# A gated scan with a two-level mixture of experts on one core: units' work due earlier, two jobs' staged weights asked for ahead of rows

## The chip, the cores and the metric

The kernel runs on one core of a Trainium2 chip. The time is the device time of one execution in microseconds (us), as the median of the runs; TensorE (PE in the profile), VectorE (DVE), ScalarE (ACT), GpSimd (POOL) and SyncE (SP, which only issues transfers here) work side by side and wait for each other by semaphores. PEld is TensorE's weight load, which runs beside the matmuls.

## The reference

A linear recurrence over time, per batch and channel, makes the tokens; each token is then sent to one of 16 experts (4 groups of 4, the largest logit in both steps), and the expert's two-layer network is weighted by the two softmax values.

```
x, f_logit: (4, 3648, 256)   lower_bound: (256)
w_group (256, 4)  w_expert (4, 256, 4)  w1 (4, 4, 256, 1024)  w2 (4, 4, 1024, 256)
f = lower_bound + (1 - lower_bound) * sigmoid(f_logit)
h = f[:, t] * h + (1 - f[:, t]) * x[:, t];  y[:, t] = h          # 14592 tokens of 256
g = argmax(y @ w_group);  e = argmax(y @ w_expert[g])
out = softmax(y @ w_group)[g] * softmax(y @ w_expert[g])[e] * (relu(y @ w1[g, e]) @ w2[g, e])
```

## The kernel before

**Units.** The 14592 tokens are cut into 29 units of 512 (the last one of 256), numbered 0 to 28. A unit's work is: a load of 1 MB (`p1_load`, into one of four `zt` tiles; units 4 to 7 use two `st` tiles instead), a tanh and two affine steps on ACT (L219, L229), one gate on DVE (L245, or L266 for some early units), two scans on DVE (L256), transposes back to rows on PE (L284) and their copies on ACT, router matmuls on PE (L303), a transpose of the logits (L316), and routing: a chain of some twenty short DVE instructions per pair of units (L330 to L389, and L655 to L706 for the choice of experts), which ends in `posi`, the place of each token in its expert's list. GpSimd then scatters the rows into the lists in DRAM (`xs`, L393).

**Jobs.** While later units are still being made, 16 A jobs (A0 to A15) each take 2 to 5 tiles of 128 tokens from the list that is fullest at a given unit (`CHOOSE`, `EARLY`: the unit at which the job's rows are cut, and its tiles). 16 B jobs later do what is left of every expert. The fifth job of the title is A4, the sixth A5, the eighth A7.

- A0 to A3 (`RAW` = 4) are raw: their weights go into `w` tiles and are used as f32 (L1071 for the first layer, L1110 for the second), 16 + 16 matmuls of 256 columns; DVE has nothing to do for them but ACT has the relus (L1074).
- From A4 on weights are staged: four loads of 512 KB go into `st` tiles (eight of them, `STG_BUFS`; `job_weights`, L963), and `job_split` makes a high f16 part on ACT (L971) and a low bf16 part on DVE (L973, called a split here). Rows come into `xr` tiles (six of them; L946), are transposed on PE (L1033) and split on ACT and DVE (L1042, L1043). The first layer is three matmuls for each block (L1097 to L1099) into `ps_m`, evicted by ACT (`hh`, L1102) and DVE (`hl`, L1103); the second layer (L1129) reads `hh` and `hl`.
- A4 and A5 have 2 tiles each and are cut at unit 10, A6 has 3 and is cut at 12, A7 has 3 and is cut at 14. Units are counted into the lists up to the cut, and their scattered rows must have landed before a job's rows are loaded.

**What sets the order.** Once the first jobs start, the units' work stands in a queue of small pieces (`bgq`). After each step of a job `bg_step` takes pieces from it at a rate: for every entry (work, mark) in the list `due`, the pieces still missing to the mark divided by the work left to that point, and the largest of these. Work is counted in steps: a raw or 2-tile job has 10, a 3-tile job 19. `marks[u]` is the place in the queue behind which job rows that are cut at unit u have been asked for. Before, `due` has an entry for every job: the mark of a job's rows is due about half a job before the job ahead of it ends; of A6 (mark 12) at 45, of A7 (mark 14) at 55, where the fourth job ends at 40. The queue of SP keeps the order in which the program asks; on PE, DVE and ACT the build's scheduler sets the order after the first job's start from the order written. `early_rows(u)` asks for the rows of the jobs cut at u; `fetch_to(n)` asks for weights until n pieces (four for each job) have been asked for; each job's preparation asks for some pieces itself, up to two ahead.

Of the kernel before, what the change touches and what calls it, by code (L numbers as in the profile page):

```python
# [22 lines left out]
EARLY = [(4, 2), (6, 2), (8, 2), (8, 2), (10, 2), (10, 2), (12, 3), (14, 3),  # L23
         (16, 4), (18, 4), (20, 4), (22, 5), (24, 5), (26, 5), (28, 5), (28, 5)]
# [11 lines left out]
RAW = 4  # L36
# [17 lines left out]
def gated_scan_moe(ctx: ExitStack, tc, zx, lower, wroute, wexp, out, S):  # L54
# [391 lines left out]
    def p1_thunks(us, groups, parts):  # L446
# [54 lines left out]
        for u in us + [us[-1] + 1]:  # L501
            seq = []
            if u <= FAST:
# [39 lines left out]
                for m in [m for m, v in ROWS_AT.items() if u == v]:  # L543
                    f = lambda m=m: early_rows(m)
                    f.mark = m
                    put(f)
# [11 lines left out]
                if u == FAST:  # L558
                    f = lambda: None
                    f.mark = "begun"  # L560
                    put(f)
                    for v in [v for v in sorted(cuts) if v <= FAST and v not in ROWS_AT]:
                        f = lambda v=v: early_rows(v)
                        f.mark = v
                        put(f)
# [122 lines left out]
    def blanks():  # L688
        while unblanked:
            j = unblanked.pop(0)  # L690
            m = 1 if EARLY[j.idx][1] == 2 else 2
            sync.dma_start(out=xs_v[NT + j.idx][bass.ds(j.e * LW + (PRE - m * P), m * P), :].rearrange("(p k) c -> p k c", k=m),
                           in_=blank[:, None, :].broadcast_to([P, m, RW]))
# [18 lines left out]
        B.tensor_tensor(out=taken, in0=taken, in1=got, op=ALU.add)  # L712

    def early_rows(u):
        for mac in macros:
            for j in mac:
                if j.kind == "A" and EARLY[j.idx][0] == u and j.idx < NE - 1:
                    job_rows(j)
        ready[0] = True
        if u == EARLY[0][0]:  # L720
            fetch_to(pptr[0] + 8)
# [118 lines left out]
    def make_job(kind, idx):  # L840
        j = Job()
        j.kind, j.idx = kind, idx
        j.len = EARLY[idx][1] * P if kind == "A" else CAPS[idx] if kind == "B" else P
        j.tiles = -(-j.len // P)
        j.chunks, j.pieces, j.cols, j.parts = [], [], [], []
        at = 0
        while at < j.len:
            rest = j.len - at
            if kind == "B":
                w = rest if rest <= UNIT else UNIT if rest >= UNIT + P else UNIT - P  # L850
            else:
                w = 2 * P if rest > 3 * P else P if rest > 2 * P else rest
            n = UNIT // w
            j.cols.append([list(range(c, min(KF, c + n))) for c in range(0, KF, n)])
            j.pieces += [(b, min(2 * P, at + w - b)) for b in range(at, at + w, 2 * P)]
            parts, b = [], at
            while b < at + w:
                m = at + w - b
                g = 1 if m > 64 else 2
                parts.append((b, min(m, P // g), g))  # L860
                b += P // g
            j.chunks.append((at, w))
            j.parts.append(parts)
            at += w
        j.raw = kind == "A" and idx < RAW
        j.wh, j.wl, j.st = {}, {}, {}
        j.hh, j.hl = {}, {}
        j.xh, j.xl = {}, {}
        return j
# [85 lines left out]
    def job_weights(j, i):  # L955
        e = job_e(j)
        if j.raw:
            w = wp.tile([P, 1024], F32, name=f"w{i}")
            sync.dma_start(out=w, in_=wexp[bass.ds(e * P, P), i * 1024:(i + 1) * 1024])
            j.wh[i], j.wl[i] = w[:, 0:512], w[:, 512:1024]  # L960
            return
        st = stg.tile([P, 1024], F32, name="st")
        sync.dma_start(out=st, in_=wexp[bass.ds(e * P, P), i * 1024:(i + 1) * 1024])  # L963
        j.st[i] = st
# [184 lines left out]
    macros = [[make_job("A", e)] for e in range(NE)]  # L1149
# [17 lines left out]
    def first_parts():  # L1167
        out = []
        for (j,), u in zip(macros, PLAN):
            half = {}  # L1170

            def begin(j=j, half=half):
                half[0] = bank("m2")
                raw2(j, 0, 0, range(KF // 2), half[0])
            fs = [lambda j=j: job_xt(j, 0)]
            fs += [lambda j=j, cs=cs: m1_step(j, 0, cs) for cs in j.cols[0]]
            fs += [begin, lambda j=j, half=half: m2_step(j, 0, 0, half[0])]
            out += [(u, f) for f in fs]
        return out

    thunks, marks = p1_thunks(list(range(NU)), GROUPS, first_parts())
# [7 lines left out]
    def bg_to(n):  # L1189
        while done[0] < n:  # L1190
            bg_pop()

    def fetch_to(n):
        while pptr[0] < min(n, len(pieces)):
            j, i = pieces[pptr[0]]
            if j.kind == "A" and j.idx not in picked:
                return
            if j.kind != "A":
                bg_to(marks["order"])
            job_weights(j, i)  # L1200
            pptr[0] += 1
        if ready[0]:
            ready[0] = False
            blanks()
# [33 lines left out]
    def work(mac):  # L1238
        return sum(len(j.chunks) * KF + sum(len(p) for p in j.parts) for j in mac)

    due = []
    at = 0
    for mi, mac in enumerate(macros):
        at += work(mac)
        if mi + 2 < len(macros):
            nxt = macros[mi + 2][0]
            due.append((at - (work(mac) // 2 if mi else 0), marks[EARLY[nxt.idx][0]] if nxt.kind == "A" else marks["order"]))
            if nxt.kind == "A" and nxt.idx >= NE - 2:
                due[-1] = (at - work(mac) // 2, marks["order"])
    now = [sum(work(mac) for mac in macros[:len(PLAN)])]  # L1250
    credit = [0.0]

# [110 lines left out]
```

## Time and profile before

| what | value |
|---|---|
| median of 3 runs (lowest, highest) | 763.11 us (760.62, 766.0) |
| the profiled execution's time | 761.96 us |
| its span, first to last instruction | 760.2 us |
| PE busy | 715.6 us (94%) |
| DVE, ACT, POOL busy | 514.6, 445.9, 296.3 us |
| TensorE clock granted, mean | 0.994 |

Some 1.8 us of the profiled execution lie outside the span. The shares are means over stages: up to about 60 us units alone are made, then the raw jobs run to about 137 us, then the A jobs beside the remaining units, and later jobs alone.

### The profile page before, as it was taken

What the parts mean: (1) busy time and instruction counts of PE and PEld (TensorE: products, weight loads), DVE (VectorE), ACT (ScalarE), POOL (GpSimd) and SP (SyncE); (2) the same over time, 40 slices, a digit from 0 to 9 for tenths busy, and PEclk for the clock granted to TensorE, in tenths of its full rate; (3) what the DMA queues carried; (4) which work ended last, traced back from release to release, by engine and by line L of the source; (5) the groups of instructions that cost most, each with busy time, mean ns of one, the idle gap of its engine ahead of it and who ended that gap; (6) DMA issues with size and microseconds to landing.
All of it is one profiled execution on the core that took longest, in us unless ns stands there. A gap on an engine that the chain in (4) does not pass through costs nothing.

```text
span 760.2 us, 17863 instructions
## 1 busy us (share of the span) xinstructions
PE 715.6 (94%) x6471; PEld 588.0 (77%) x6471; DVE 514.6 (68%) x1086; ACT 445.9 (59%) x827; POOL 296.3 (39%) x314
## 2 busy tenths in 40 slices
PE   3569999998899999999999999999999999999995
PEld 1457888886788888888999676867778886777895
DVE  6899758999799976495556754644644645755660
ACT  6567767887577855454545644544544545655651
POOL 3656267668567764632222121312122121123232
PEclk9999999999999999999999999999999999999998
DMA  8978789989888873657994470617155345655520
GB/s 326 413 255 292 243 351 289 408 316 310 289 258 292 242 211 117 170 146 189 222 241 106 113 189 29 169 43 188 47 155 131 114 133 168 196 174 170 168 65 23
DMA packets 100410, 151.35 MB, mean 199 GB/s; under 512 B 60203, under 2 KB 70206, under 8 KB 97504
## 3 DMA queue, kind: packets, MB, share of 16 engines
q1 hardware_dynamic: 85792, 102.84, 46.1%
q0 software_dynamic: 11408, 30.02, 10.7%
q10 hardware_dynamic: 3120, 17.34, 6.7%
q8 instruction: 51, 0.84, 0.5%
q14 instruction: 39, 0.32, 0.1%
HBM read 112.49 MB, written 37.96 MB: 198 GB/s over the span
## 4 chain that ended last, share of the span: by engine, by line
PE 71%; DVE 11%; issue 8%; DMA 3%; POOL 3%; ACT 2%; another core or an unknown queue 1%; SPq 1%; POOLq 0%; DVEq 0%
PE ps_m L1129 28%; PE ps_m L1099 7%; PE ps_m L1097 7%; PE ps_m L1098 7%; PE ps_m L1110 4%; PE ps_m L1071 4%; PE ps_p L1097 3%; PE ps_p L1098 3%; PE ps_p L1099 3%; PE ps_p L284 3%; POOL out_dram L1143 3%; DVE h L256 2%; DVE w L973 1%; PE ps_p L303 1%; DVE hl L1103 1%
## 5 line engine op out<-in xcount | busy, mean ns | idle before, releaser
L1129 PE MATMUL ps_m<-w,hh 128*128 128x256 f16 (+5 forms) x1260 | 218.9, 268 | 1.3 <-issue 1.3
L1129 PE MATMUL ps_m<-w,hl 128*128 128x256 f16 (+4 forms) x740 | 188.5, 267 | 0.6 <-issue 0.6
L973 DVE TENSOR_TENSOR w<-st,w 128x1024 bf16<-128x1024 f32 x112 | 135.8, 1219 | 68.2 <-ACT w L971 66.7
L393 POOL DMA_INDIRECT xs<-rows,posi x114 | 138.2, 1212 | 87.6 <-ACT rows L288 25.6
L1143 POOL DMA_INDIRECT out_dram<-o,info x67 | 71.6, 1069 | 244.1 <-ACT o L1141 226.6
L1129 PE MATMUL ps_m<-w,rows 128*128 128x256 f16 (+5 forms) x880 | 133.8, 267 | 0.3 <-issue 0.3
L1129 PEld LDWEIGHTS <-hh 128*128 128x128 f16 (+7 forms) x1260 | 117.9, 101 | 15.6 <-issue 3.3
L971 ACT CAST w<-st 128x1024 f16<-128x1024 f32 x112 | 116.1, 1047 | 17.6 <-PE ps_m L1129 12.5
L1097 PE MATMUL ps_m<-xh,w 128*128 128x256 f16 (+9 forms) x494 | 120.4, 256 | 2.5 <-DVE hl L1103 2.4
L1099 PE MATMUL ps_m<-xh,w 128*128 128x256 f16 (+9 forms) x494 | 120.3, 256 | 0.8 <-issue 0.8
L1098 PE MATMUL ps_m<-xl,w 128*128 128x256 bf16 (+9 forms) x494 | 120.3, 256 | 0.0
L1103 DVE SCALAR_TENSOR_TENSOR hl<-ps_m,hh 128x512 bf16<-128x512 f32 (+7 forms) x107 | 71.1, 671 | 40.6 <-ACT hh L1102 24.7
L1098 PEld LDWEIGHTS <-w 128*128 128x128 f16 x800 | 78.3, 98 | 25.3 <-issue 3.7
L1097 PEld LDWEIGHTS <-w 128*128 128x128 f16 x800 | 78.3, 98 | 23.2 <-issue 1.6
L1099 PEld LDWEIGHTS <-w 128*128 128x128 bf16 x800 | 78.3, 98 | 22.8 <-issue 0.4
L1143 POOL DMA_INDIRECT out_dram<-o,meta x47 | 53.4, 1136 | 101.8 <-ACT o L1141 69.1
L1129 PEld LDWEIGHTS <-rows 128*128 128x128 f16 (+4 forms) x880 | 81.6, 101 | 10.0 <-issue 0.6
L1102 ACT ACTIVATE hh<-ps_m 128x512 f16<-128x512 f32 (+7 forms) x107 | 63.3, 594 | 37.1 <-PE ps_m L1099 32.1
L1141 ACT ACTIVATE o<-ps_m,info 128x256 f32<-128x256 f32 (+4 forms) x67 | 31.1, 463 | 91.5 <-PE ps_m L1129 75.8
L1129 PEld LDWEIGHTS <-hl 128*128 128x128 bf16 (+4 forms) x740 | 70.8, 101 | 9.1 <-issue 1.9
L256 DVE TENSOR_TENSOR_SCAN h<-zt,h 128x512 f32<-128x512 f32 (+3 forms) x48 | 56.6, 1191 | 0.5
L1103 DVE SCALAR_TENSOR_TENSOR hh<-ps_p,rows 128x512 bf16<-128x512 f32 (+7 forms) x30 | 17.6, 586 | 45.4 <-ACT rows L1102 45.3
(203 smaller groups left out, 1183.4 us busy)
## 6 DMA issues: line engine op xcount, KB each, us to landing
st<-in_wexp_dram SPq DMA_DIRECT2D x112, 512.0 KB
zt<-in_zx_dram ACTq DMA_DIRECT2D x16, 1024.0 KB
w<-in_wexp_dram SPq DMA_DIRECT2D x16, 512.0 KB
xs<-blank SPq DMA_DIRECT2D x26, 258.0 KB
zt<-in_zx_dram SPq DMA_DIRECT2D x6, 1024.0 KB
st<-in_zx_dram SPq DMA_DIRECT2D x8, 512.0 KB
xr<-xs SPq DMA_DIRECT2D x12, 258.0 KB
xr<-xs SPq DMA_DIRECT2D x16, 129.0 KB
```

The source lines that it names most:

```text
L256: sn = nc.vector.tensor_tensor_scan(out=h[:, k, c0 - a:c1 - a], data0=ff[:, k, c0 - a:c1 - a], data1=uu[:, k, c0 - a:c1 - a], initial=init ...
L393: sc = nc.gpsimd.indirect_dma_start(out=xs_v[G["t0"] + t][:, :], out_offset=bass.IndirectOffsetOnAxis(ap=R["posi"][:, t:t + 1], axis=0), i ...
L971: nc.scalar.copy(j.wh[i], j.st[i])
L973: nc.vector.tensor_tensor(out=j.wl[i], in0=j.st[i], in1=j.wh[i], op=ALU.subtract)
L1097: nc.tensor.matmul(po, w1_at(j.wh, k, c), xh[:, k], start=(k == 0), stop=False)
L1098: nc.tensor.matmul(po, w1_at(j.wh, k, c), xl[:, k], start=False, stop=False)
L1099: nc.tensor.matmul(po, w1_at(j.wl, k, c), xh[:, k], start=False, stop=(k == KD - 1))
L1102: eviction[0] = nc.scalar.activation(hi, pv, AF.Relu).ins
L1103: nc.vector.scalar_tensor_tensor(out=h_at(j.hl[ch], cs, slice(0, w)), in0=pv, scalar=0.0, in1=hi, op0=ALU.max, op1=ALU.subtract)
L1129: nc.tensor.matmul(pm[i * q:i * q + n, 0:dw], h_at(h[ch], [c], ts)[:, 0], w2_at(w, c)[:, i * dw:(i + 1) * dw], start=(c == 0 and s == 0), ...
L1141: nc.scalar.activation(o[s, 0:dw], pm[s, 0:dw], AF.Copy, scale=lt.bitcast(F32)[s, r, 1:2])
L1143: nc.gpsimd.indirect_dma_start(out=out_v[out_n[0]].rearrange("n (g d) -> (n g) d", g=g), out_offset=bass.IndirectOffsetOnAxis(ap=lt[s, r, ...
```

## The change

Two additions. In `early_rows`, at the cut of the fifth job (unit 10), weights are asked for up to piece 24, which is all four pieces of A4 and A5, before their rows. And `due` gets one more entry: mark 14, behind which A7's rows have been asked for, is due at the end of the fourth job (40 steps in place of 55), which raises the rate at which pieces of the units' work are taken during the raw jobs. Nothing is computed that was not computed before, and no instruction of the jobs or the units is added or left out. Lines from 715 on are two higher in the changed file, those from 1250 on three.

```diff
     def early_rows(u):
+        if u == EARLY[RAW][0]:
+            fetch_to(4 * (RAW + 2))
         for mac in macros:
             for j in mac:
                 if j.kind == "A" and EARLY[j.idx][0] == u and j.idx < NE - 1:
...
             if nxt.kind == "A" and nxt.idx >= NE - 2:
                 due[-1] = (at - work(mac) // 2, marks["order"])
+    due.append((sum(work(mac) for mac in macros[:RAW]), marks[EARLY[RAW + 3][0]]))
     now = [sum(work(mac) for mac in macros[:len(PLAN)])]
```

How the order moves. On SP, at the loads of the fifth job's rows (`st` is a staged weight piece, `xr` the rows, `posA` the place of the list's cut), before:

```order
L963 DMA st<-in_wexp_dram 128x1024
L896 ISA
L896 TENSOR_LOAD posA
L896 ISA x2
L946 ISA
L946 REGISTER_ALU
L946 DMA xr<-xs 128x258
```

and now, five more pieces of weights ahead of the same load (the last three of them shown):

```order
L965 ISA
L965 DMA st<-in_wexp_dram 128x1024
L965 ISA
L965 DMA st<-in_wexp_dram 128x1024
L965 ISA
L965 DMA st<-in_wexp_dram 128x1024
L898 ISA
L898 TENSOR_LOAD posA
L898 ISA x2
L948 ISA
L948 REGISTER_ALU
L948 DMA xr<-xs 128x258
```

Before, three of the eight pieces of A4 and A5 stood ahead of these rows; now all eight do.

On PE, at the end of the fourth job (second layer L1110, now L1112) and the first matmul of the fifth, before:

```order
L316 MATMUL ps_p<-ident,rs 128x128
L1110 MATMUL ps_m_1899<-w_1294,hh 128x256 x4
L1110 MATMUL ps_m_1899<-w_1511,hl 128x256 x2
L1110 MATMUL ps_m_1929<-w_1294,hh 128x256 x2
L1110 MATMUL ps_m_1899<-w_1511,hl 128x256 x2
L1110 MATMUL ps_m_1929<-w_1294,hh 128x256 x2
L1110 MATMUL ps_m_1929<-w_1511,hl 128x256 x4
L284 MATMUL ps_p<-ident,h 128x128 x4
L1097 LDWEIGHTS w_1770
```

and now:

```order
L1112 MATMUL ps_m_2080<-w_1312,hh 128x256 x2
L316 MATMUL ps_p<-ident,rs 128x128
L284 MATMUL ps_p<-ident,h 128x128 x4
L1112 MATMUL ps_m_2053<-w_1533,hl 128x256 x2
L303 MATMUL ps_p<-h,wr 32x128 x8
L284 MATMUL ps_p<-ident,h 128x128 x4
L1112 MATMUL ps_m_2080<-w_1533,hl 128x256 x2
L1099 LDWEIGHTS w_1835
```

More of the units' transposes and routers stand among the raw jobs' matmuls: ahead of the fifth job's first matmul PE has the routers of units 0 to 14 before, and of units 0 to 16 now.

On DVE, around the fifth job's first evictions (`hl`, L1103, now L1105; `w<-st` is a split, L245 a unit's gate), before:

```order
L375 RECIPROCAL rows<-s_1925 128x4 x2
L973 TENSOR_TENSOR w_1983<-st,w_1983 128x1024
L245 SCALAR_TENSOR_TENSOR zt<-zt 128x1024
L973 TENSOR_TENSOR w_1988<-st,w_1988 128x1024
L256 SCALAR_TENSOR_TENSOR h<-zt,h 128x512
L973 TENSOR_TENSOR w_2047<-st,w_2047 128x1024
L1103 SCALAR_TENSOR_TENSOR hl<-ps_m_1966,hh 128x512
L973 TENSOR_TENSOR w_2052<-st,w_2052 128x1024
L1103 SCALAR_TENSOR_TENSOR hl<-ps_m_2030,hh 128x512
```

and now:

```order
L375 RECIPROCAL rows<-s_2113 128x4 x2
L1105 SCALAR_TENSOR_TENSOR hl<-ps_m_2132,hh 128x512
L245 SCALAR_TENSOR_TENSOR zt<-zt 128x1024
L975 TENSOR_TENSOR w_2150<-st,w_2150 128x1024
L975 TENSOR_TENSOR w_2155<-st,w_2155 128x1024
L1105 SCALAR_TENSOR_TENSOR hl<-ps_m_2171,hh 128x512
```

The sixth job's splits, which stood ahead of the fifth job's first evictions, now stand between and behind them. Counted over the whole order: ahead of the fifth job's second `hl` there are 12 gates of L245 and 8 splits before, 14 gates and 6 splits now; ahead of the 18th `hl` 17 gates and 20 splits before, 18 gates and 20 splits now; ahead of the 34th 21 gates before and 23 now; from about the 41st on the two orders are level.

## Rows read from the trace of the kernel before

**Rows 1.** The page: PE over the span, and busy tenths in 40 slices.
```profile
PE 715.6 (94%) x6471; PEld 588.0 (77%) x6471; DVE 514.6 (68%) x1086; ACT 445.9 (59%) x827; POOL 296.3 (39%) x314
...
PE   3569999998899999999999999999999999999995
```

**Rows 2.** Windows: busy us (x instructions) by engine, clock, DMA share, GB/s.
```profile
60.00:80.00 20.00, 19.77 (x136) 15.67 (x137) 16.36 (x50) 14.76 (x34) 11.64 (x12) 1.00 0.79 266
80.00:100.00 20.00, 20.00 (x155) 16.66 (x154) 15.09 (x31) 13.99 (x33) 7.21 (x11) 1.00 0.83 286
100.00:120.00 20.00, 20.00 (x136) 16.78 (x135) 13.20 (x30) 13.28 (x27) 13.64 (x14) 1.00 0.83 295
120.00:140.00 20.00, 20.00 (x142) 16.96 (x141) 16.87 (x35) 17.06 (x31) 14.63 (x17) 1.00 1.01 350
140.00:160.00 20.00, 20.00 (x221) 17.86 (x219) 19.90 (x46) 16.35 (x31) 9.40 (x10) 1.00 1.02 400
160.00:180.00 20.00, 18.18 (x192) 15.43 (x189) 19.76 (x40) 16.16 (x34) 16.85 (x16) 1.00 0.92 276
180.00:200.00 20.00, 17.91 (x186) 14.44 (x184) 15.51 (x27) 11.79 (x22) 16.05 (x17) 1.00 0.93 316
200.00:220.00 20.00, 17.86 (x176) 15.14 (x177) 18.78 (x41) 16.75 (x32) 12.51 (x13) 1.00 0.81 275
157.40:213.20 55.80, 49.76 (x530) 41.32 (x529) 49.96 (x109) 40.81 (x80) 40.44 (x42) 1.00 0.91 296
220.00:240.00 20.00, 20.00 (x206) 17.57 (x205) 19.74 (x43) 14.93 (x30) 13.79 (x17) 1.00 0.89 288
260.00:280.00 20.00, 19.00 (x196) 16.71 (x195) 18.43 (x43) 13.47 (x27) 15.19 (x15) 1.00 0.67 213
```

**Rows 3.** Timeline of PE, 160 to 210 us: instructions with idle time ahead, and its releaser.
```profile
161.54 0.27 PE L1097 MATMUL ps_m<-xh,w 128*128 128x256 f16 x1 [0.47 <-DVE hl L1103]
...
174.67 0.33 PE L316 MATMUL ps_p<-ident,rs 128*128 128x128 f32 x1 [1.04 <-DVE both L381]
...
187.20 0.27 PE L1129 MATMUL ps_m<-w,hh 128*128 128x256 bf16 x1 [0.38 <-issue]
...
200.96 0.66 PE L284 MATMUL ps_p<-ident,h 128*128 128x128 f32 x4 [1.29 <-DVE both L381]
...
207.73 0.27 PE L1097 MATMUL ps_m<-xh,w 128*128 128x256 f16 x1 [0.65 <-DVE hl L1103]
```

**Rows 4.** Groups of DVE, 157.4 to 213.2 us: count, busy us, mean ns, idle before.
```profile
L256 DVE TENSOR_TENSOR_SCAN h<-zt,h 128x512 f32<-128x512 f32 (+1 forms) x11 | 12.6, 1152 | 0.0
L973 DVE TENSOR_TENSOR w<-st,w 128x1024 bf16<-128x1024 f32 x9 | 10.6, 1220 | 0.0
L1103 DVE SCALAR_TENSOR_TENSOR hl<-ps_m,hh 128x512 bf16<-128x512 f32 x14 | 9.4, 674 | 0.0
L245 DVE SCALAR_TENSOR_TENSOR zt<-zt 128x1024 f32<-128x1024 f32 x5 | 6.1, 1212 | 0.0
L1043 DVE TENSOR_TENSOR xl<-ps_p,xh 128x512 bf16<-128x512 f32 (+1 forms) x4 | 2.5, 617 | 1.0 <-issue 0.6 <-ACT xh L1042 0.4
```

**Rows 5.** Waits in 60 to 140 us: us in total, times, longest.
```profile
DVE zt L245 <- ACT zt L229: 7.2, 5, 2.6
```

**Rows 6.** Timeline of SP's queue (start, us), and PE's transposes of the fifth job's rows.
```profile
95.13 1.48 SPq L963 DMA_DIRECT2D st<-in_wexp_dram  x3
113.14 3.33 SPq L946 DMA_DIRECT2D xr<-xs  x4
...
121.66 7.79 SPq L963 DMA_DIRECT2D st<-in_wexp_dram  x6
...
126.62 0.63 PE L1033 MATMUL ps_p<-ident,xr 128*128 128x128 f32 x4
```

**Rows 7.** The page's part on DMA issues: KB of one staged piece.
```profile
st<-in_wexp_dram SPq DMA_DIRECT2D x112, 512.0 KB
```

**Rows 8.** Timeline of PE ahead of the first job: a wait for a routing step.
```profile
54.91 0.21 PE L419 MATMUL ps_p<-oh16f,upto 128*128 128x64 bf16 x1 [3.00 <-DVE oh16f L407]
```

## The prediction

> **What bounds the kernel now.** I read the page first, then the windows, then PE's timeline where PE stops, then DVE by groups. The page: PE is busy for 715.6 us of a span of 760.2, so all that a reordering can win is inside 44.6 us of idle time. The row of tenths says where it lies: the first three slices, the last one, and two slices of 8 in the tenth and eleventh place, which is about 171 to 209 us [rows 1]. The change touches neither the first slices (its first moved instruction on PE stands among the raw jobs) nor the last; what it can reach is the dip. The windows show it: PE is full from 80 to 160 us, then busy for 18.18, 17.91 and 17.86 us of three windows of 20, so 6.05 us idle; the granted clock is 1.00 in every one of these rows, the level of 2.4 GHz, so it is not the clock [rows 2].
>
> A stop is longer than it looks. A matmul's end in the trace is modelled, 0.27 us after its start, although they follow each other faster, so the beginning of each stop is covered. The weight loads give another measure: 17.86 us in the full window 140 to 160, that is 0.893 of it, which over 60 us would be 53.6 us; the three windows have 45.0, so about 8.6 us of PE's work are missing there [rows 2]. The Trainium skill says the same of such rows (Perfetto Trace Analysis, Identifying the Most-Contended Engine): matmul busy time is no measure, weight-load busy time is. By it the dip is worth 8.6 us and not 6.05, and this trace agrees, since counting by weight loads finds more than the idle column.
>
> Who ends the stops: DVE, four times of the five rows shown, by `hl` (0.47, 0.65) or by `both`, a routing step (1.04, 1.29). One kind is different: around 187 to 192 us PE stops six times for up to 0.38 us (one row stands for them) with nothing that the profile shows [rows 3]. And DVE is full just there: 19.90 and 19.76 us of 20 from 140 to 180. From 60 to 140, during the raw jobs, which need nothing of it, it is busy for 16.36 + 15.09 + 13.20 + 16.87 = 61.5 of 80 us, so 18.5 idle [rows 2]. So PE bounds the whole, and DVE bounds the stretch from A4 to A7.
>
> **The change part by part.**
>
> *Rate of the units' work.* Price of a unit on DVE: from 157.4 to 213.2 us DVE is busy for 49.96 us [rows 2]; the jobs' part is 10.6 (splits) + 9.4 (`hl`) + 2.5 (`xl`) = 22.5; five gates say that five units went by, so (49.96 - 22.5) / 5 = 5.5 us for a unit. Two scans and a gate alone are 2 x 1.15 + 1.21 = 3.5, the lower bound; the rest is routing. A split is 10.6 / 9 = 1.18 us [rows 4].
>
> The counts of the order (in the section on the change) then say what moves on DVE. (a) Ahead of A4's second `hl`: two units more and two splits less, 2 x 5.5 - 2 x 1.18 = 8.6 us more work, into a stretch with 18.5 us of idle DVE. (b) Between the second and the 18th `hl`, which is the dip: four units in place of five, but 14 splits in place of 12: 5.5 - 2.4 = 3.1 us less. A5's splits come back out of the raw jobs into A4, so the relief is a good third of a naive two units (11 us). (c) Between the 18th and the 34th `hl`: five units in place of four, 5.5 us more. (d) After that it is given back.
>
> What each is worth. For (a), 61.5 + 8.6 = 70.1 of 80 us is 88% of DVE; the nearest row, 120 to 140 us, has 84% and no idle PE, so I take 0; from above it is bounded by the third rival. PE itself takes two units' transposes and routers earlier and has them no more later: nothing in sum. Part of DVE's idle time there is waiting for ACT's affine step, 7.2 us in five waits [rows 5], and it shrinks if ACT gets its pieces earlier too. (b) is on the path, since PE stops for DVE there: -3.1 us; from below it is bounded by the whole 8.6. (c) falls on a DVE with little air: 19.74 us of 20 are busy from 220 to 240, 18.43 from 260 to 280 [rows 2], so idle time is about 0.3 and 1.6 us. Five and a half microseconds more there cost PE between 0 and 3.6 (5.5 less the 1.9 shown). But in the row from 220 to 240 PE had no idle time with DVE at 99%: DVE full is not yet DVE late, if it comes into the stretch ahead. I take 1.0, nearer to that row.
>
> *Weights in front of rows.* Five more issues of SP stand ahead of A4's rows. Three took 1.48 us at 95.13, so five take 2.5, and SP has nothing from 96.6 to 113.14 but the wait for those rows' scatters [rows 6]; the issues hide in it, as long as the scatters are what the rows wait for. Rows asked for at 113.14 are transposed at 126.62, so they have 13 us to spare as well. The weights come earlier: but from 100 to 160 us PE never waited, so nobody waited for weights, and earlier is worth 0. A7's rows now stand ahead of A6's last piece of weights on SP, and wait for a free `xr` tile that A3 holds; what queues behind is weights which are split half a job or more later. 0 as well.
>
> *Pool and ACT.* Two units more are eight scatters more in the raw stage on a GpSimd that is busy for 47 of 80 us there, and ACT is at 59 of 80 [rows 2]. Neither is full; 0.
>
> **Sum:** 0 - 3.1 + 1.0 = -2.1 us. The profiled execution took 761.96 (span 760.2 and 1.76 around it), which would become 759.9; it lies 1.15 below the median of 763.11, which becomes **761.0 us**.
>
> **The rivals.**
>
> 1. *All of the dip goes: 754.5.* PE's loss there may be a chain: DVE late by a little, a bank of `ps_p` freed late, the routing step late in turn (the two `both` rows). If 3.1 us less demand and two units' head start break the chain, all 8.6 us return and (c) stays free. For it: DVE was at 99% and PE at 100% from 140 to 160, so the balance is near. Against it: the stops of 187 to 192 us are not DVE's, and (c).
>
> 2. *Loads get in each other's way: 767.6.* 5 x 512 KB are 2.62 MB [rows 7], at the 400 GB/s of 140 to 160 us [rows 2] 6.6 us of all DMA engines, pulled forward to where two more unit loads of 1 MB also come. If units' loads are late by all of it once, PE stands 6.6 us in a transpose: -2.1 + 6.6 = +4.5. The DMA share is 0.79 to 0.83 from 60 to 120 us, which speaks for room, and 1.01 from 120 to 140, which speaks against it [rows 2]. The Trainium skill (DMA: Bandwidth & Descriptors, Issuing engines are not separate DMA queues) states that SP's, ACT's and GpSimd's transfers interleave on the same 16 engines, so a weight asked for early is paid by a unit's load. By that rule this rival is the outcome; no row of the kernel before shows a unit's load that PE waited for after 60 us.
>
> 3. *Slower: 773.0.* In the raw stage PE's queue now has routing steps and transposes closer together, and each stands ahead of matmuls that could run. Where units ran that close, ahead of the first job, PE stood 3.00 us for one routing step of DVE [rows 8]. Some four routing steps stand between the first raw job and A4's first matmuls; if each stops PE for as long, 4 x 3.0 = 12 us, less 2.1, is +9.9. It decides when DVE's spare time in the raw stage is not spare, because its instructions wait for ACT in order: from about 88% on the next row up is a full DVE, and a full DVE is what made the dip.
>
> 4. *Nothing moves: 763.1.* The rate rises, but the scheduler and the splits that come back leave DVE as far behind at A6 as before, and (b) and (c) cancel.
>
> **How the numbers follow.** Chances: the forecast 0.50 (757 to 765), the first rival 0.17, the second 0.10, the third 0.13, the fourth 0.10. One per cent, about what a measurement of this kernel can tell from no change, is 7.6 us: faster than 755.5 is the first rival, 0.17; slower than 770.7 the third, 0.13; the rest, 0.70, is within it. The range from 754 to 768 takes in the forecast with its bounds and all rivals but the third; with a tail beyond the first it leaves out 0.18.
>
> **What would show it.** In the windows of the changed kernel DVE must rise to about 88% from 60 to 140 us with PE still full: a PE below 19.5 of 20 there is the third rival, with a releaser on DVE, or the second, with transposes that wait for scans whose `zt` came late. Between 160 and 220 PE's idle time should fall from 6.05 to about 3 to 4 us, and weight loads rise from 45.0 by some 3. Between 220 and 280 DVE should be full and PE lose about 1 us more. SP should ask for all eight pieces of A4 and A5 before the wait for rows, and those rows should still arrive well ahead of their transposes. The sum is wrong if PE's loss in the dip was not DVE's work but the order within it: then the count of units does not tell its size.

## The result and the profile after

| | before | changed |
|---|---|---|
| median of 8 runs (lowest, highest) | 762.98 us (760.16, 766.25) | 771.12 us (768.3, 775.92) |
| ratio, 95% interval | | 1.0101 (1.0066 to 1.0135) |
| span of the profiled execution | 760.2 us | 769.4 us |
| TensorE clock granted, mean | 0.994 | 0.978 |

The change made the kernel 1% slower: 8.1 us between the medians (5 to 10 by the interval). The time lies outside the range of the prediction (754 to 768), and nearest to its third rival (773.0).

The page of the changed kernel, where it answers to [rows 1] (PE over the span, busy tenths in 40 slices, and the granted clock in tenths):

```profile
PE 720.4 (94%) x6467; PEld 589.1 (77%) x6471; DVE 516.6 (67%) x1086; ACT 447.5 (58%) x827; POOL 295.7 (38%) x314
...
PE   3569999889989999999999999999999999999996
...
PEclk9859999999999999999999999999999999999999
```

The granted clock of the kernel before, in the same form:

```profile
PEclk9999999999999999999999999999999999999998
```

The dip of the tenth and eleventh slices is gone, but 8s stand in the eighth, ninth and twelfth: the weak place has moved ahead, to about 135 to 175 us. The low clock of the second and third slice is not the change's doing: the kernel before with A5's splits moved to GpSimd (below), an edit that bears on later jobs alone, has 0.74 and 0.67 from 20 to 40 and 40 to 60 us. PE's busy time is 4.8 us longer for the same matmuls; the part of it that lies behind 60 us shows in the windows, of the same stretches as [rows 2] (busy us by engine, clock, DMA share, GB/s):

```profile
60.00:80.00 20.00, 19.41 (x142) 15.10 (x143) 15.89 (x52) 14.15 (x32) 12.25 (x12) 1.00 0.80 276
80.00:100.00 20.00, 20.00 (x157) 16.64 (x156) 14.39 (x29) 14.05 (x34) 6.89 (x9) 1.00 0.80 258
100.00:120.00 20.00, 20.00 (x151) 16.11 (x150) 15.62 (x38) 13.48 (x31) 15.07 (x19) 1.00 1.03 411
120.00:140.00 20.00, 19.21 (x129) 16.14 (x128) 16.39 (x32) 15.03 (x29) 14.46 (x15) 1.00 0.87 269
140.00:160.00 20.00, 18.00 (x146) 14.63 (x145) 17.16 (x35) 15.49 (x29) 15.08 (x16) 0.91 0.77 279
160.00:180.00 20.00, 16.64 (x176) 14.21 (x174) 19.93 (x44) 16.63 (x28) 10.42 (x11) 0.91 1.01 381
180.00:200.00 20.00, 20.00 (x213) 17.59 (x212) 17.43 (x30) 13.75 (x30) 14.13 (x13) 1.00 0.88 281
200.00:220.00 20.00, 18.29 (x172) 14.33 (x169) 17.69 (x41) 12.58 (x25) 12.81 (x14) 1.00 0.88 292
220.00:240.00 20.00, 19.55 (x188) 17.21 (x188) 19.47 (x43) 15.05 (x28) 12.66 (x13) 1.00 0.80 253
260.00:280.00 20.00, 19.30 (x189) 17.02 (x187) 17.00 (x33) 11.85 (x24) 13.83 (x13) 1.00 0.65 209
```

Two things are to be seen. From 60 to 140 us DVE is busy for 15.89 + 14.39 + 15.62 + 16.39 = 62.3 us; it was 61.5 [rows 2], and 70.1 were forecast. By 140 us hardly any of the 8.6 us of work that stand earlier in the order have been done (in the second profile of the changed kernel the sum is 61.0). And 140 to 160, where PE was full before, has 18.00 us of PE, 14.63 of weight loads (before 17.86), and a granted clock of 0.91.

PE's stops in that stretch, from its timeline, where [rows 3] had the dip's:

```profile
126.56 0.66 PE L284 MATMUL ps_p<-ident,h 128*128 128x128 f32 x4 [0.79 <-ACT rows L286]
...
148.94 0.61 PE L1131 MATMUL ps_m<-w,hh 128*128 128x256 f16 x4 [0.46 <-ACT hh L1104]
...
151.09 0.27 PE L1099 MATMUL ps_m<-xh,w 128*128 128x256 f16 x1 [1.54 <-DVE hl L1105]
...
165.15 0.27 PE L1099 MATMUL ps_m<-xh,w 128*128 128x256 f16 x1 [1.25 <-DVE hl L1105]
...
171.00 0.22 PE L1099 MATMUL ps_m<-xh,w 128*128 128x128 f16 x1 [0.91 <-DVE hl L1105]
```

Between the raw jobs' end and the end of A5 PE waits mostly for evictions, `hh` on ACT and `hl` on DVE. In this execution the clock falls after the stops; windows of 3 us (columns as above):

```profile
147.00:150.00 3.00, 2.10 (x18) 1.62 (x16) 2.90 (x6) 2.65 (x4) 2.84 (x4) 1.00 0.76 306
150.00:153.00 3.00, 1.91 (x12) 1.43 (x12) 2.94 (x6) 3.00 (x6) 2.39 (x3) 0.76 0.27 96
153.00:156.00 3.00, 3.00 (x20) 2.44 (x19) 3.00 (x4) 3.00 (x6) 2.39 (x3) 0.67 0.46 124
```

PE was busy for 2.10 and 1.91 us of 3, and then had 0.76 and 0.67 of its clock on average, which is a part of each window at the lower of the two levels, 1.2 GHz. The same happens at 171 to 177 (0.68 and 0.76). The four windows are short of (0.24 + 0.33 + 0.32 + 0.24) x 3 = 3.4 us of full clock. The first of these two falls is not there in a second execution of the same program, although PE stops there at least as much:

```profile
147.00:150.00 3.00, 1.73 (x16) 1.46 (x14) 2.86 (x7) 3.00 (x5) 2.84 (x3) 1.00 0.80 325
150.00:153.00 3.00, 2.10 (x20) 1.87 (x20) 2.98 (x5) 3.00 (x6) 2.21 (x3) 1.00 0.27 95
153.00:156.00 3.00, 2.21 (x21) 1.81 (x19) 3.00 (x5) 3.00 (x7) 2.57 (x2) 1.00 0.60 170
```

The second fall is there again (0.52 and 0.91 at 171 to 177). That execution took 769.41 us, so most of the loss does not hang on the fall at 150 us.

Why A4's first evictions are late shows in the timeline of all engines where A4 begins. These rows are picked out of it:

```profile
140.76 0.27 PE L1099 MATMUL ps_m<-xh,w 128*128 128x256 f16 x1
...
141.16 0.42 DVE L348 TENSOR_TENSOR_SCAN scn<-rmask,oh 128x128 bf16<-128x128 bf16 x1
...
142.94 0.19 PE L355 MATMUL ps_p<-scn,tri 128*128 128x16 bf16 x1
...
144.07 0.19 DVE L381 TENSOR_TENSOR both<-ps_p,both 128x32 f32<-128x32 f32 x1 [2.49 <-PE ps_m L1101]
...
145.49 1.20 DVE L245 SCALAR_TENSOR_TENSOR zt<-zt 128x1024 f32<-128x1024 f32 x1
...
146.73 2.46 DVE L256 TENSOR_TENSOR_SCAN h<-zt,h 128x512 f32<-128x512 f32 x2
...
147.35 1.06 ACT L219 ACTIVATE zt<-zt 128x1024 f32<-128x1024 f32 x1 [1.25 <-DMA zt<-in_zx_dram]
...
148.31 0.58 ACT L1104 ACTIVATE hh<-ps_m 128x512 f16<-128x512 f32 x1
...
150.38 0.66 DVE L1105 SCALAR_TENSOR_TENSOR hl<-ps_m,hh 128x512 bf16<-128x512 f32 x1
...
154.36 0.68 DVE L1105 SCALAR_TENSOR_TENSOR hl<-ps_m,hh 128x512 bf16<-128x512 f32 x1
```

And A4's second `hl` in the kernel before:

```profile
142.20 0.68 DVE L1103 SCALAR_TENSOR_TENSOR hl<-ps_m,hh 128x512 bf16<-128x512 f32 x1
```

PE starts A4's first block at 140.76. A routing chain of two units stands in DVE's queue ahead of that block's eviction. Its matmul L355 needs `scn`, which DVE has at 141.58, but stands on PE behind some twenty of A4's matmuls and starts at 142.94. DVE, which takes its instructions in order, stands still for 2.49 us; then come the rest of the chain, a gate and two scans, and the `hl` that PE waits for comes at 150.38. On ACT the first `hh` stands behind a tanh that waits 1.25 us for a unit's load. The second `hl` of A4 ends at 155.0; before, at 142.9.

### The profile page after: what moved, and what is told of

It is laid out like the page before. It is cut to its first block, busy times and chain, and to the rows that moved or that the text cites. A ratio compares the mean times of both kernels' runs of the same rounds, so it can differ in the third digit from the quotient of the medians.

```text
span 769.4 us, 17860 instructions
## 1 busy us (share of the span) xinstructions
PE 720.4 (94%) x6467; PEld 589.1 (77%) x6471; DVE 516.6 (67%) x1086; ACT 447.5 (58%) x827; POOL 295.7 (38%) x314
## 4 chain that ended last, share of the span: by engine, by line
PE 38%; issue 35%; DVE 11%; POOL 10%; ACT 2%; DMA 2%; another core or an unknown queue 1%; POOLq 1%; SPq 0%; DVEq 0%; ACTq 0%
PE ps_m L1131 13%; POOL out_dram L1145 9%; PE ps_m L1101 5%; PE ps_m L1099 4%; PE ps_m L1100 4%; PE ps_p L284 3%; PE ps_m L1112 3%; PE ps_m L1073 2%; DVE h L256 2%; DVE w L975 2%; PE ps_p L303 2%; DVE hl L1105 1%; PE ps_p L1035 1%; DMA zt<-in_zx_dram 1%; DMA xs<-rows,posi 1%
## 5 line engine op out<-in xcount | busy, mean ns | idle before, releaser
L393 POOL DMA_INDIRECT xs<-rows,posi x114 | 133.0, 1167 | 91.7 <-ACT rows L288 26.4
L1099 PE MATMUL ps_m<-xh,w 128*128 128x256 f16 (+9 forms) x494 | 122.0, 259 | 5.6 <-DVE hl L1105 4.5
L1101 PE MATMUL ps_m<-xh,w 128*128 128x256 f16 (+9 forms) x494 | 122.1, 259 | 0.6 <-issue 0.4
L1100 PE MATMUL ps_m<-xl,w 128*128 128x256 bf16 (+9 forms) x494 | 122.0, 259 | 0.4 <-issue 0.2
L1105 DVE SCALAR_TENSOR_TENSOR hl<-ps_m,hh 128x512 bf16<-128x512 f32 (+7 forms) x107 | 71.2, 673 | 45.8 <-ACT hh L1104 29.9
L1105 DVE SCALAR_TENSOR_TENSOR hh<-ps_p,rows 128x512 bf16<-128x512 f32 (+7 forms) x30 | 17.6, 587 | 45.5 <-ACT rows L1104 36.5
```

Source lines behind the costliest of these rows:

```text
L393: sc = nc.gpsimd.indirect_dma_start(out=xs_v[G["t0"] + t][:, :], out_offset=bass.IndirectOffsetOnAxis(ap=R["posi"][:, t:t + 1], axis=0), i ...
L1099: nc.tensor.matmul(po, w1_at(j.wh, k, c), xh[:, k], start=(k == 0), stop=False)
L1100: nc.tensor.matmul(po, w1_at(j.wh, k, c), xl[:, k], start=False, stop=False)
L1101: nc.tensor.matmul(po, w1_at(j.wl, k, c), xh[:, k], start=False, stop=(k == KD - 1))
L1105: nc.vector.scalar_tensor_tensor(out=h_at(j.hl[ch], cs, slice(0, w)), in0=pv, scalar=0.0, in1=hi, op0=ALU.max, op1=ALU.subtract)
```

## The experiments

Every ratio is against the kernel before, run on the same chip in the same round. Theory 1: the new due entry costs the time. Theory 2: the weights in front crowd the transfers. A third theory, that ACT's wait for a free `o` tile sets it off (2.71 us ahead of 125.55, then PE's stop of 0.79 at 126.56), could not be tried by itself: seven such tiles in place of five do not fit beside the rest. Traces of two runs below speak against it: with the rate alone, and with the splits early, there is no such wait for a DMA and no stop of PE at this place, and the loss is the same (1.0105 and 1.0099).

**Weights only, rate only.** The two additions, one at a time.

```diff
-    due.append((sum(work(mac) for mac in macros[:RAW]), marks[EARLY[RAW + 3][0]]))
```

> Only the first addition: the eight pieces of A4 and A5 ahead of A4's rows, the old rate. PE, DVE and ACT have word for word the order of the kernel before; only SP's queue differs. Theory 1 (the new due entry does it: units' steps that stand closer together at the end of the raw jobs make evictions and routing late, PE stops in A4 and A5, and its clock falls): this kernel is the kernel before, 762 to 764 us, ratio 0.998 to 1.002, and PE full from 80 to 160. Theory 2 (the weights asked for earlier crowd the transfers, units' loads come late and everything behind them): most of the loss is here, 768 to 772, with unit loads that land later than before between 95 and 140 us.

Measured: 761.55, ratio 0.9999 (0.9974 to 1.0025).

```diff
-        if u == EARLY[RAW][0]:
-            fetch_to(4 * (RAW + 2))
```

> Only the second addition: A7's rows due at 40 steps, weights asked for as before. Theory 1: all of the loss is here, 769 to 773 us, ratio 1.008 to 1.013, with PE stops on ACT and DVE between 125 and 172 us as in the changed kernel. Theory 2: without the weights in front the loads are back in time: 762 to 765, PE full from 80 to 160.

Measured: 771.36, ratio 1.0105 (1.0062 to 1.0149). Theory 2 has fallen, the rate does all of it. The windows of the kernel with the weights alone show PE as full as before, with 394 GB/s from 100 to 120 us where there were 295 [rows 2]:

```profile
100.00:120.00 20.00, 20.00 (x137) 16.74 (x136) 12.88 (x30) 13.31 (x28) 13.89 (x14) 1.00 1.02 394
...
140.00:160.00 20.00, 20.00 (x224) 17.86 (x223) 19.90 (x46) 16.46 (x31) 10.13 (x9) 1.00 1.01 383
```

**How much of the rate.** A7's rows due later than in the changed kernel (40 steps). The 55 of the kernel before lies half a job before the end of A5, at 60, which is the job two places ahead of A7.

```diff
-    due.append((sum(work(mac) for mac in macros[:RAW]), marks[EARLY[RAW + 3][0]]))
+    due.append((sum(work(mac) for mac in macros[:RAW]) + 8, marks[EARLY[RAW + 3][0]]))
```

> Both additions, but A7's rows due at 48 steps, half way between 40 and what was due before (55). Ahead of A4's second hl DVE has 17 gates and 6 splits (before 16 and 8, changed 18 and 6). Theory 1 as a matter of degree: about half of the loss, 766 to 768. Theory 1 as a threshold (PE stops only when two units' routing meets A4's first evictions): 761 to 764. Theory 2: the weights are still in front, so 768 to 772.

Measured: 771.07, ratio 1.011 (1.0068 to 1.0151). With + 12 in place of + 8:

> Both additions, A7's rows due at 52 steps (before it was 55, changed 40, and 48 cost as much as 40). Ahead of A4's second hl DVE has 16 gates and 8 splits, as before. Theory 1 as a threshold between 48 and 55: 762 to 764 here if the units' place before A4's first evictions is what counts, since it is as before; 768 or more if any move of the units' steps costs the same.

Measured: 764.18, ratio 1.0018 (0.9995 to 1.004). It is no matter of degree between 40 and 48, and neither form of theory 1 (766 to 768, or 761 to 764) had the 771.07 at 48. At 52 as many units stand ahead of A4 as before, 15 by their routers on PE; at 48 there are 16, in the changed kernel 17.

**The same programs once more.**

> The changed kernel once more, for a second profile of the same program. Theory 1 and every theory that lays the loss on the new order: the fourth job ends again 8 to 10 us later than in the kernel before, PE stops again on ACT and DVE between 125 and 172 us, and the clock falls again in A4. If instead the low clock of the first 60 us and the stops without a releaser (one instruction every 0.7 us) are chance of one execution, they are elsewhere or gone here, while the time stays at 769 to 773.

Measured: 769.41 (one run); A3 ends at 145.4 us (145.6 in the first profile, 136.7 before), and PE's stops in A4 and A5 are there again, 0.61 to 2.18 us long:

```profile
150.90 0.27 PE L1099 MATMUL ps_m<-xh,w 128*128 128x256 f16 x1 [2.18 <-DVE rows L375]
...
154.91 0.28 PE L1131 MATMUL ps_m<-w,hl 128*128 128x256 f16 x1 [0.79 <-DVE hl L1105]
...
157.77 0.27 PE L1099 MATMUL ps_m<-xh,w 128*128 128x256 f16 x1 [0.61 <-DVE hl L1105]
...
164.95 0.27 PE L1099 MATMUL ps_m<-xh,w 128*128 128x256 f16 x1 [1.25 <-DVE hl L1105]
...
170.80 0.22 PE L1099 MATMUL ps_m<-xh,w 128*128 128x128 f16 x1 [1.89 <-DVE hl L1105]
```

The clock did not fall again in A4: it is 1.00 from 140 to 160 us, where the first profile has 0.91.

> The kernel due at 48 once more, for a second profile. If the stops without a releaser belong to the program, they stand again at the router of A6 (about 192 us) and in A4 (143, 169 us), and A6 ends again some 12 us behind the kernel before. If they are chance of one execution, they are gone, and the 10 us lie in stops on DVE or ACT, in A4 and A5 as with two units ahead, or the time is near 763.

Measured: 769.55 (one run). The stops without a releaser stand at the same places as in its first profile: in A4, and in a unit's router inside A6. From PE's timeline of this second profile:

```profile
144.94 0.27 PE L1101 MATMUL ps_m<-xh,w 128*128 128x256 f16 x1 [1.16 <-issue]
146.35 0.27 PE L1099 MATMUL ps_m<-xh,w 128*128 128x256 f16 x1 [1.14 <-issue]
...
193.71 0.59 PE L303 MATMUL ps_p<-h,wr 128*32 128x128 f32 x2 [1.85 <-issue]
```

So with one unit more ahead of A4 the loss has another form than with two: matmuls that should follow each other at 0.11 us start 0.7 or 1.4 us apart, for some 3 us at 143, 2.5 at 168 and 5.5 at 190; together PE is idle for some 8 us in them. What holds them is not in the trace.

**Unit loads earlier.** Theory 4: units are paced by their loads.

```diff
-                seq += [lambda u=u: (p1_load(u + AHEAD - 1), u + 1 in us and p1_ta(u + 1))]
+                seq += [lambda u=u: (p1_load(u + AHEAD - 1), p1_load(u + AHEAD), u + 1 in us and p1_ta(u + 1))]
```

> The changed kernel, but from unit 10 on each unit's load is asked for one unit earlier (three units ahead, in the same four zt tiles). Theory 4 (units in the raw jobs are paced by their loads, which land 10 us after they are asked for, just when the tanh needs them, so that a higher rate only lets PE stand): ACT's waits for zt go, and 763 to 766. Theory 1 (PE is paced by its own order, and the loads have nothing to do with it): 769 to 773.

Measured: 778.31, ratio 1.0204 (1.0167 to 1.0241).

> The kernel before with the same earlier loads, as the other half of that comparison. No theory has unit loads as a wait of the kernel before (ACT has 13 to 16 us from the load to the tanh there), so 760 to 764; the splits of A5 move back behind A4's first evictions as in the changed kernel (6 ahead of the second hl in place of 8), with the units where they were: if those splits alone set off the stops in A4, 766 to 771.

Measured: 769.98, ratio 1.008 (1.0059 to 1.01). Earlier loads cost about 0.8 to 1% in both: theory 4 has fallen, and by the opposite sign. In the second kernel ACT's cast of a staged piece waits for that piece, which it did not before (how much of the 0.8% comes by this wait is not shown; PE also has stops without a releaser there, from 195 to 202 us):

```profile
132.78 1.04 ACT L971 CAST w<-st 128x1024 f16<-128x1024 f32 x1 [4.33 <-DMA st<-in_wexp_dram]
```

**The splits alone.** Theory 5: A5's splits that come back into A4. Theory 6: the units' work ahead of A4 was moved in the order, not in time.

`low_parts` are A4's `hl` instructions; `...` stands for the rest of the line.

```diff
+        pin = j.kind == "A" and j.idx == RAW + 1 and i >= 2 and len(low_parts) >= 2
+        with tc.issue_after(low_parts[1]) if pin else ...
             nc.vector.tensor_tensor(out=j.wl[i], in0=j.st[i], in1=j.wh[i], op=ALU.subtract)
```

> The kernel before with one thing of the change alone: the last two splits of A5 are held behind A4's second hl (6 splits ahead of it, as in the changed kernel; 16 gates, units and loads as before). Theory 5 (every kernel that was slower has 6 splits there and every one that was not has 8: the splits that come back into A4 meet a DVE that is full, and hl is late): 766 to 771. Theory 6 (the units' work was moved ahead of A4 in the order but not in time: DVE and PE get it done no sooner, and A4 only waits for it; the splits are a small part): 762 to 765.

Measured: 762.21, ratio 1.0001 (0.9978 to 1.0024). And the other way round, in the changed kernel:

```diff
                 if j.kind == "A" and j.idx == RAW and ch == 0:
+                    for _ in range(4):
+                        if not (getattr(q[0], "held", False) and live[0] >= 3):
+                            q.popleft()()
```

> The changed kernel with A5's four splits written ahead of A4's first block, so that 18 gates and 8 splits stand ahead of A4's first hl. Theory 5: DVE has nothing of A5 left inside A4, and the time falls to 763 to 766. Theory 6: A4 now waits for the splits as well, 770 to 775.

Measured: 770.03, ratio 1.0099 (1.0068 to 1.0129). Theory 5 has fallen on both sides. In the last kernel the small stops of A4 have run together into two; PE's timeline:

```profile
150.11 1.04 PE L1131 MATMUL ps_m<-w,hh 128*128 128x256 f16 x4 [4.40 <-ACT hh L1104]
...
154.16 0.37 PE L1099 MATMUL ps_m<-xh,w 128*128 128x256 f16 x1 [1.97 <-DVE w L975]
```

**DVE relieved.** A5's splits on GpSimd.

```diff
-            nc.vector.tensor_tensor(out=j.wl[i], in0=j.st[i], in1=j.wh[i], op=ALU.subtract)
+            (nc.gpsimd if j.kind == "A" and j.idx == RAW + 1 else nc.vector).tensor_tensor(out=j.wl[i], ...)
```

> The changed kernel with A5's four splits on GpSimd in place of DVE (4.9 us of DVE's work taken out of A4, and four longer instructions into GpSimd's queue of scatters). If a full DVE in A4 and A5 is what makes PE stop there (theories 1 and 5), 763 to 767, with stops on hl shorter by half. Theory 6: DVE has less to do, but the units ahead of A4 still have to pass PE and DVE first: 768 to 771. GpSimd's scatters may come later for it, which could cost 1 to 4 us more in either.

Measured: 773.62, ratio 1.0136 (1.0106 to 1.0166).

> The same of the kernel before. If DVE bounds the stretch from A4 to A7, as the prediction had it, 4.9 us less of it there are worth 2 to 4 us: 758 to 761. If the stops in the dip are the order and not the load, 761 to 764; if GpSimd's scatters suffer, 764 to 768.

Measured: 764.75, ratio 1.0037 (1.0012 to 1.0063). 4.9 us less on DVE bring neither kernel anything; both lose some 3 us, and in the changed one PE now stops 1.00 and 1.57 us for splits of GpSimd. This does not show what DVE's load alone is worth, since slower splits came with it (four took 8.4 us on GpSimd).

**More units, and fewer.**

```diff
-    due.append((sum(work(mac) for mac in macros[:RAW]), marks[EARLY[RAW + 3][0]]))
+    due.append((sum(work(mac) for mac in macros[:RAW]) + -6, marks[EARLY[RAW + 3][0]]))
```

> The changed kernel with A7's rows due at 34 steps: 18 routers ahead of A4's first matmul (before 15, due at 48 16, changed 17), 18 gates and 8 splits ahead of A4's first hl. Theory 6 with a price for each unit (some 3 to 5 us of PE and DVE that A4 waits for and that come back only in part): 772 to 777. If the loss is one step that is taken when PE stops in A4 at all (the stops and the clock, whatever the count): 769 to 772.

Measured: 775.35, ratio 1.016 (1.0133 to 1.0186). Theory 7 is that of the phase: units are routed in pairs, and the time is lost when a whole routing chain stands on DVE ahead of A4's first evictions, whatever the count. With - 4:

> The changed kernel with A7's rows due at 36 steps: 18 routers ahead of A4's first matmul (before 15, changed 17), but on DVE only the second half of a pair's routing chain stands between A4's rows and its first hl and the next chain begins behind the third hl, nearly as in the kernel before. Theory 7 (phase: PE stops when a whole chain with its two trips through ACT and PE stands ahead of A4's first evictions): 761 to 765, A4's first evictions without a stop of PE. Theory 6 (each unit ahead of A4 has its price): 772 to 777, between the changed kernel and the one due at 34.

Measured: 763.92 on a chip on which the kernel before takes 751.86, ratio 1.0159 (1.0132 to 1.0185). Theory 7, the phase, has fallen: with the phase of the kernel before, three units cost what they cost without it. This also says that the stops at A4's first evictions are where the loss shows in the changed kernel, and need not be what it hangs on: here PE is busy for 19.98 us from 140 to 160 and for 59.5 of 60 from 180 to 240, but it stops ahead of A4, again from 162 to 166 us, and later (2.13 us for an `hl` at 252.52):

```profile
120.00:140.00 20.00, 17.79 (x123) 13.98 (x125) 18.71 (x33) 17.79 (x34) 16.90 (x16) 1.00 0.87 280
140.00:160.00 20.00, 19.98 (x193) 17.20 (x194) 19.76 (x40) 15.80 (x29) 14.51 (x14) 1.00 0.93 305
160.00:180.00 20.00, 16.92 (x185) 14.86 (x183) 20.00 (x44) 16.17 (x32) 14.26 (x14) 1.00 0.99 358
...
240.00:260.00 20.00, 16.53 (x144) 13.52 (x143) 16.08 (x23) 14.24 (x25) 10.74 (x10) 0.91 0.68 214
```
```profile
138.02 0.66 PE L284 MATMUL ps_p<-ident,h 128*128 128x128 f32 x4 [1.36 <-DVE both L381]
```

Slower rates, of the kernel before:

```diff
+            if nxt.kind == "A" and RAW <= nxt.idx < 8:
+                due[-1] = (due[-1][0] + 6, due[-1][1])
```

> The kernel before with the rows of A4 to A7 due six steps later: 15 gates and 8 splits ahead of A4's first hl (before 16 and 7). Theory 6 in the other direction: A4 starts 2 to 4 us earlier and waits less, but the units are later for A6 and A7: 759 to 764. If the order before A4 is on an edge on one side only: 761 to 764. If units are late in the dip: 765 to 770.

Measured: 769.7, ratio 1.0088 (1.0057 to 1.012); PE stops 2.12 us at 129.09 and 1.75 at 156.09, and has stops without a releaser at 193 to 197. With + 2:

> The kernel before with the rows of A4 to A7 due two steps later (the one six steps later cost 7 us): 15 routers ahead of A4 as before, the second half of a chain ahead of the first hl, the next chain behind the fourth. Theory 7: 761 to 764. If the kernel before is on an edge in the slower direction as well, so that any shift costs: 767 to 771.

Measured: 753.47 against 751.86, ratio 1.0021 (1.0004 to 1.0038). Ordered by the units whose router stands ahead of A4 on PE: 15 units, the normal loads and DVE's splits give 0.9999 to 1.0021 (four kernels; 1.0088 at the slowest rate), 16 units 1.011, 17 units 1.0099 to 1.0105 (three), 18 units 1.0159 and 1.016 (two). Theory 6 is left, that units written ahead of A4 are done no sooner and have to be waited for, but its price for each unit is not: one unit costs as much as two, and three cost half as much again. No version beats the kernel before.

## Why the prediction was wrong, point by point

**The step that failed** is term (a): 8.6 us more work ahead of A4's second `hl`, taken as 0 because DVE had 18.5 us of idle time in the raw jobs, with PE's two units "nothing in sum". What the runs show in its place, worked out below: from A0's end to A9's the changed kernel takes 6.4 us longer. The cover was not there. Most of DVE's idle time in the raw jobs is waiting in order, not room. In the kernel before it waited from 60 to 140 us for ACT's affine step [rows 5], for logits (4.1 us) and for PE (3.9), and work that is written earlier waits for the same things: in the changed kernel, in the same window, for the affine step (3.4 us), for logits (2.2), for `both` (1.6), then 2.49 us for `both` at 144.07. Gates 16 to 20 of the units end there at 133.4, 146.7, 152.2, 168.1 and 181.5 us, where those of the same number ended at 137.1, 148.6, 162.6, 172.2 and 182.2 before: ahead by 4, 2, 10, 4 and 0.7 us; gate 12, early in the raw jobs, ends 3.8 us later than before. Meanwhile A4's second `hl` came 12.1 us later.

The ends of the jobs (start of the last `o` on ACT, us) say where it went. The kernel with the weights alone has the order of the kernel before on PE, DVE and ACT, and less of the stops without a releaser; the second profile of the changed kernel has less of them too, so these two are compared. They come from two chips, on which the kernel before takes 761.11 and 762.86 us.

| | A0 | A3 | A4 | A5 | A6 | A7 | A8 | A9 | A15 |
|---|---|---|---|---|---|---|---|---|---|
| before | 81.4 | 136.7 | 160.4 | 174.5 | 195.3 | 223.4 | 245.8 | 273.3 | 436.9 |
| weights only | 81.0 | 136.3 | 160.1 | 174.0 | 193.0 | 216.8 | 242.4 | 269.9 | 433.6 |
| changed | 82.9 | 145.6 | 170.6 | 185.3 | 204.4 | 229.3 | 256.7 | 281.2 | 445.6 |
| changed again | 82.7 | 145.4 | 169.4 | 185.1 | 205.0 | 226.7 | 255.1 | 278.0 | 443.3 |
| difference of the two | 1.7 | 9.1 | 9.3 | 11.1 | 12.0 | 9.9 | 12.7 | 8.1 | 9.7 |

From A0's end to A9's the changed kernel takes 195.3 us in place of 188.9, and in the first two profiles 198.3 in place of 191.9: 6.4 us more in both pairs. What lies outside of this stretch is not shown to be the change's: A0's end lies between 79.1 and 86.9 us in all profiles, and from A9's end to the end of the span the two profiles of the changed kernel take 488.2 and 489.6 us, both kernels of the other order 486.9, and the kernel with the splits late, level in time, 488.0.

From A0's end to A3's, 7.4 us are added. PE's groups in that stretch, for the kernel with the weights alone (81.0 to 136.3 us) and the changed one (82.9 to 145.6), line, shape, count, busy us, mean ns:

```profile
L284 PE MATMUL ps_p<-ident,h 128*128 128x128 f32 x51 | 7.9, 276 | 0.0
L303 PE MATMUL ps_p<-h,wr 128*32 128x128 f32 x96 | 3.9, 279 | 0.0
```
```profile
L284 PE MATMUL ps_p<-ident,h 128*128 128x128 f32 x66 | 10.4, 279 | 0.8 <-ACT rows L286 0.8
L303 PE MATMUL ps_p<-h,wr 128*32 128x128 f32 x128 | 5.2, 279 | 0.0
...
L1099 PE MATMUL ps_m<-xh,w 128*128 128x256 f16 x8 | 2.2, 272 | 0.0
```

Two units' transposes (16, of which 15 are in the records), routers (32) and transposes of logits (2) more, and 24 matmuls of A4's first layer that were not there before. Those 24 follow each other at 0.11 us, 2.6 in all, and would make A4 that much shorter. The stop at 126.56 is 0.8. The rest, 7.4 - 2.6 - 0.8 = 4.0, is two units on a full PE, 2.0 us each; the two groups alone have (10.4 - 7.9) + (5.2 - 3.9) = 3.8 us more, and with one unit more (due at 48) the stretch takes 57.2 us in both profiles, 1.9 longer. The prediction wrote "PE itself takes two units' transposes and routers earlier and has them no more later: nothing in sum". The first half is shown; the second holds only if the 4.0 come back later.

From A3's end to A6's the changed kernel loses 2.9 us more, although 2.6 of A4 were done: some 5.5 us. PE's stops there on DVE are the five of the second profile, 0.61 to 2.18 us, together 6.7, against 2.3 in all of the same jobs with the weights alone. From A6's end to A9's it gets 3.9 back, which is about the two units' 4.0. In the first two profiles the same stretches give 0.2 lost and 1.2 got back (the kernel before has stops without a releaser in A6); so the 6.4 in sum is firmer than its parts, and that the 4.0 come back in full is not shown.

**(b), the relief of the dip, -3.1 us: neither shown nor excluded.** The sign that was set for it does not tell. Weight loads from 160 to 220 us are 14.21 + 17.59 + 14.33 = 46.1 us in the changed kernel, where 45.0 were and some 48 were forecast; but they are 47.7 in its second profile, and 48.8 with the weights alone, which has the order of the kernel before. The dip of 8.6 us, read from one execution, was thus in part that execution's. From A5's end to A7's the changed kernel takes 44.0 and 41.6 us, against 48.9 before and 42.8 with the weights alone; but the two units' work on PE may be missing from this stretch, so what is saved there need not be DVE's. That DVE bounds A4 to A7 as a sum of work is not borne out by any run; stops by order and stops without a releaser are what the traces show.

**(c), +1.0:** PE's idle time is 0.45 from 220 to 240 and 0.70 from 260 to 280, against 0 and 1.00; but A8 takes 27.4 and 28.4 us in the two profiles of the changed kernel, 22.4 before and 25.6 with the weights alone, and A9 evens it out: A8 and A9 together take 51.9 and 51.3 us, against 49.9 and 53.1. A cost of 1.0 is within this spread; its size is not shown.

**The weights in front: 0.** Right (0.9999), and the second rival with it is out for this change. Its mechanism exists all the same: a megabyte of a unit asked for earlier goes with staged weights that are late, in a kernel that is 0.8% slower (loads ahead). Here the weights had room: 394 GB/s from 100 to 120 us, beside a full PE. The rule of the Trainium skill that the prediction weighed (DMA: Bandwidth & Descriptors, Issuing engines are not separate DMA queues: transfers of all issuers interleave on the same engines) agrees with the 4.33 us of the loads ahead; that the sharing costs anything did not follow from it for the weights.

**Pool and ACT: 0.** Wrong for ACT: its `hh` stood behind `o` and a tanh, and PE waited 0.46 us for it at 148.94 (not in the second profile), and 4.40 us when the splits were put first.

**The rivals.** The third gave 773.0 from four stops of 3.0 us within the raw jobs. Its sign and its reason were right, instructions in order and a DVE whose spare time is not spare; its place and its price were not, so that its number came near is luck. In the raw jobs PE stops for only 0.8 us; the price is two units of PE's own time and some 5.5 us in A4 to A6, less what comes back. The first and the fourth, faster and no change, are out by the measured time. The third's chance, 0.13, was too low: the row against which (a) was priced, 84% busy with no idle PE, has PE full, and a full PE is what the moved work must pass. That was readable in [rows 2].

**Open** are the stops without a releaser, which make up most of the loss with one unit ahead, and so why one unit costs as much as two; why three units cost the same with stops at A4's first evictions and without; and whether the slowest rate loses by units that come late or by stops without a releaser.

## What to carry to other kernels

Idle time of an engine that works in order, beside another that is full, need not be room: before work is priced at nothing, follow one unit of it through every engine that it passes, and ask which instruction it will stand in front of when it is late. A rate that brings work forward moves it in the order; here DVE had been busy for only 0.8 us more by 140 us, of 8.6 that were brought forward, and the rest then stood ahead of the next stage's first evictions. Take a second profile before a dip is sized: here two executions with one order on PE, DVE and ACT differed by 3.8 us of weight loads in 60. Try a step to either side as well: here 15 units ahead of A4 are level over a small stretch of rates, and both directions out of it cost 1%.

## What was not expected of the hardware

A stop of PE can be paid twice, but is not always: after 2.10 us busy of 3 the granted clock was 0.76 and 0.67 in the next two windows of 3 us; with 4.40 and 1.97 us of stops close together it was 0.75 over the whole stretch from 140 to 160 us, in the kernel with the splits early; and in the second execution of the changed kernel, busy for 1.73, 2.10 and 2.21 us of 3 in the same place, it stayed at 1.00.

Matmuls without a wait in the trace can start 0.7 or 1.4 us apart in place of 0.11, for 3 to 6 us. In two executions of one program these places were the same; in the kernel before and the one with the weights alone, which have one order on PE, one has such a place at 187 to 192 us [rows 3] and the other only single stops, the longest 0.76 at 198.60. Nothing here shows what they are.
